# Scores and state products of a decayed linear attention on 32-column quarters of TensorE

## The chip, the cores and the metric

One core of a Trainium2 chip runs the whole kernel. The metric is the device time of one execution in microseconds (us); lower is better. A kernel is given by the median of its runs, and one execution is taken with a profile, from which every row below comes. TensorE is called PE, its weight loads PEld, VectorE DVE, ScalarE ACT, GpSimd POOL, and SyncE, which issues the transfers, SP.

## The reference

4 sequences, 8 heads, 768 tokens, head size 48. Each head carries a complex 48 x 48 state with a decay for each row and token, and the result goes through a two-layer network with a sigmoid gate:

```python
for t in range(S):
    new_re = ar * S_re - ai * S_im
    new_im = ar * S_im + ai * S_re
    kv = einsum('bhd,bhe->bhde', k[:, :, t], v[:, :, t])
    S_re, S_im = new_re + kv, new_im
    y[:, :, t] = einsum('bhd,bhde->bhe', q[:, :, t], S_re)
x = y as (3072 tokens, 384)
h = x @ w_in          # 384 x 2048
out = (h * sigmoid(1.702 * h)) @ w_out
```

## The kernel before, in words

**Tiling.** The 3072 tokens are 12 units of 256 tokens, three to a sequence; a unit has two chunks of 128 tokens (`c`), and a chunk handles 8 heads in two halves of four (`hh`). `prepare(u)` turns the decays of a unit into factors by scans, logarithms and sines on DVE and ACT, multiplies q and k by them, and sends the products by DMA into `qkh`, where each head has its 48 real parts in partitions 0 to 47 and its 48 imaginary parts in 64 to 111. `attend(u)` (L677 to L778) is the attention of a unit. `moe(n)` (L784 to L866) is the network, for a block of one or two units: `hidden` (L807, matmul at L814) and `project` (L833, matmul at L845). The first two blocks hold one unit and work in fp32; the other five hold two units and split each fp32 value into two fp32r parts, so that three products stand for one.

**The attention on TensorE.** Every fp32 matmul stands in the trace as two records, and each record has a weight load.
- `scores` (L702, matmul at L707): for each half of four heads, keys against queries. Keys come in two pieces of 64 (`x`); a piece's output stands in a 64-partition half of the PSUM tile `p_ps`, turned by head, and only queries from the first key of the piece on are computed: 128 columns for the first piece, 64 for the second. 8 matmuls, 16 records. DVE then multiplies by a causal mask (`pm`, L711), which has two layouts for the two ways in which the halves are turned.
- `mix` (L718, matmul at L733): values and old state against masked scores and queries, into `x_ps`; four heads each write their own 32 partitions. In three parts `r`, the last with twice the matmuls. ACT reads `x_ps` (L742), DVE the rest of it (L746).
- `turn` (L761, transpose at L763): two heads' keys transposed into `kz_ps`, copied by ACT to `kt` (L766).
- `zed` (L753, matmul at L757): transposed keys against values, the new state's products; each head has two matmuls of 48 weight columns, at output partitions 0 and 64. 8 matmuls, 16 records. DVE adds the result to the state `st` (L772, L776).

The instruction's form names the part of the array in use: 128\*128 and 112\*128 for the network and the transposes, 128\*64 for `scores`, 128\*48 for `zed`, 128\*32 for `mix`.

**Values.** `vts` holds the values of a chunk, padded, and behind them a second copy for the four odd heads, with rows rolled by 64 keys, so that they fit the turned scores. It is loaded by one DMA for each chunk (L699).

**The order of the work.** Nothing runs in the order in which it is written. `add(engine, duration, rank, function, r=, w=, kind=)` enters each step in a `Plan` with a duration written by hand and the names that it reads and writes. `order()` (L307) makes 100 rounds for each of 12 settings in `PARTS`: a forward list schedule over the five engines, a backward one for due times, ranks moved towards the due times; the order with the lowest modelled time is issued. The model charges PE `CHANGE` = 0.09 us where the next step's `kind` differs from the last one's; `stay` makes the choice of the next PE step prefer the same kind. Before the change there are two kinds: `"r"` for the fp32r network, and `None` for all else. `lag` (L83) is the delay from a step's end to its reader on another engine, 0.13 us, or 0.22 us if the reader is PE.

```python
for x in range(2):
    for j in range(4):
        h, lo = 4 * hh + j, HL * x
        to = HL * ((x + j) % 2)
        mm(p_ps[to : to + HL, j, lo:L], lhsT=at(h, 1, c)[:, lo : lo + HL], rhs=at(h, 0, c)[:, lo:L], ...)
```

Of the kernel before, what the change touches and what calls it, by code (L numbers as in the profile page):

```python
# [21 lines left out]
P = 128  # L22
L = 128
HL = 64
T = 256
# [28 lines left out]
SCRATCH = 1024  # L54

# [27 lines left out]
def lag(a, b):  # L83
    return LAG if b != "PE" else 0.0 if a == b else LAG_PE


class Plan:
# [31 lines left out]
    def forward(self, rank, stay):  # L119
# [10 lines left out]
        kinds, kind = self.kinds, None  # L130
# [5 lines left out]
        while done < len(ops):  # L136
# [29 lines left out]
            elif e == "PE":  # L166
                pick = min(can[e], key=lambda x: x[0] + (stay if kinds[x[1]] != kind else 0.0))
            else:
                pick = can[e][0]
# [16 lines left out]
            else:  # L186
# [92 lines left out]
    def time(self, order, load):  # L279
# [6 lines left out]
        kinds, kind = self.kinds, None  # L286
        for n in order:
# [11 lines left out]
            if e == "PE":  # L299
                dur += CHANGE if kinds[n] != kind else 0.0  # L300
                kind = kinds[n]
# [36 lines left out]
REMAP = 4.0  # L338
# [4 lines left out]
def attention_moe(ctx: ExitStack, tc: tile.TileContext, qk_in, v, a_in, w_in, w_out, qn, kn, vn, an, bn, out):  # L343
# [9 lines left out]
    mask = sb.tile([P, 2, P], F32, name="mask")  # L353
# [18 lines left out]
    vts = [sb.tile([P, H * VP + H // 2 * 2 * E0], F32, name=f"v{i}") for i in range(2)]  # L372
# [25 lines left out]
    nc.gpsimd.tensor_copy(out=mask[0:HL, 1, :], in_=mask[HL:P, 0, :])  # L398
    nc.gpsimd.tensor_copy(out=mask[HL:P, 1, :], in_=mask[0:HL, 0, :])
# [63 lines left out]
    def convert(n):  # L463
# [13 lines left out]
        add("SP", 2.19, rk - 4, lambda: dma(out=raw.bitcast(I32), in_=(w_in if m == "A" else w_out)[j].bitcast(I32)),  # L477
# [51 lines left out]
    def prepare_part(u, i, a, b, np_, mag, den, rec, sp, qm, th, *keys):  # L529
# [26 lines left out]
        z = 2 * C * P * 4 / 360e3  # L556
# [91 lines left out]
        for x, (dst, kd, fac, kf) in enumerate(((rv, "qr", cs, k_cs), (qv, "qk", t, k_th))):  # L648
# [3 lines left out]
            if u == i == 0 and x == 1:  # L652
                for k in range(WARM):
                    add("PE", 0.43, -WARM + k, lambda k=k, dst=dst: mm(  # L654
# [19 lines left out]
    def attend(u):  # L674
# [22 lines left out]
        for c in range(2):  # L697
            vt, kv = vts[c], f"v{c}"
            add("SP", 0.96, rk(4 * c) - 5, lambda vt=vt, c=c: dma(out=vt, in_=v[u, c]), w=[kv])  # L699
# [504 lines left out]
```

## Time and profile before

| | |
|---|---|
| median of 3 runs | 594.53 us (592.7 to 594.9) |
| the profiled execution | 593.85 us, its span 592.1 us |
| busy: PE, DVE, ACT, POOL | 94%, 79%, 47%, 4% of the span |
| records on PE | 4828, and as many weight loads |

A page of the profile gives the busy time of each engine, the chain of work that ended last, and groups of instructions by line with count, busy time and mean duration. Matmuls are pipelined, and a record's duration is longer than the step from its start to the next one's start; steps are therefore read from the timeline, as differences of starts. The timeline merges neighbouring records of one line and one pair of tiles, and shows one row with their count.

### The profile page before, as it was taken

How to read it: one execution, taken by the hardware profiler on the slowest of the kernel's cores; microseconds unless marked ns; L12 is line 12 of the kernel's file. 1: busy time of each engine (PE TensorE's matmuls, PEld its weight loads, DVE VectorE, ACT ScalarE, POOL GpSimd, SP SyncE). 2: the span in 40 equal slices, each digit the busy share in tenths (PEclk: the TensorE clock that was granted, in tenths of full speed). 3: DMA queues.
4: the chain of work that ended last, by engine and by line, in shares of the span. 5: the costliest groups of instructions: out<-in, count | busy, mean ns of one | idle time of the engine just before them, and what ended most of it. 6: DMA issues, size and time to landing. Idle time of an engine off the chain costs nothing.

```text
span 592.1 us, 11952 instructions
## 1 busy us (share of the span) xinstructions
PE 554.8 (94%) x4828; PEld 449.8 (76%) x4828; DVE 466.3 (79%) x826; ACT 276.4 (47%) x428; POOL 22.4 (4%) x75
## 2 busy tenths in 40 slices
PE   0389999999999999999999999999999999999997
PEld 0368888888788878787887787877787878878885
DVE  7999989988898977797978787977979954554333
ACT  7878677965537327237364246345346321111110
POOL 5001001000100000000000000000000000000000
PEclk9999999999999999999999999999999999999999
DMA  8478792747454192247085257286184372241111
GB/s 333 141 243 321 203 245 79 134 138 133 153 114 98 28 212 87 77 104 186 14 153 175 69 136 221 61 135 200 62 177 151 76 147 84 66 125 55 44 41 68
DMA packets 30890, 78.30 MB, mean 132 GB/s; under 512 B 4208, under 2 KB 7024, under 8 KB 30832
## 3 DMA queue, kind: packets, MB, share of 16 engines
q1 hardware_dynamic: 30832, 77.52, 48.8%
q8 instruction: 38, 0.62, 0.5%
q14 instruction: 20, 0.16, 0.1%
HBM read 53.87 MB, written 4.72 MB: 99 GB/s over the span
## 4 chain that ended last, share of the span: by engine, by line
PE 69%; DMA 13%; DVE 11%; ACT 3%; issue 2%; SPq 2%; DVEq 0%; ACTq 0%
PE h_ps L814 27%; PE o_ps L845 26%; PE x_ps L733 6%; DMA raw_w<-in_w_in_dram 4%; PE p_ps L707 4%; DMA raw_w<-in_w_out_dram 3%; PE kz_ps L763 3%; DMA raw<-in_w_out_dram 2%; PE kz_ps L757 2%; DMA raw<-in_w_in_dram 2%; DVE qk L461 1%; PE h_ps L654 1%; DMA qkh<-qr 1%; DVE pm L711 1%; DVE fit L877 1%
## 5 line engine op out<-in xcount | busy, mean ns | idle before, releaser
L826 ACT ACTIVATE g<-h_ps 128x512 f32<-128x512 f32 x80 | 47.4, 599 | 148.0 <-PE h_ps L814 138.8
L845 PE MATMUL o_ps<-gh,hiU 128*128 128x512 f32 x240 | 96.2, 401 | 0.0
L814 PE MATMUL h_ps<-xhi,hiA 128*128 128x512 f32 x240 | 95.6, 398 | 0.7 <-ACT xhi L742 0.6
L845 PE MATMUL o_ps<-gl,hiU 128*128 128x512 f32 x240 | 93.7, 391 | 0.0
L814 PE MATMUL h_ps<-xlo,hiA 128*128 128x512 f32 x240 | 93.6, 390 | 0.1
L845 PE MATMUL o_ps<-gh,loU 128*128 128x512 f32 x240 | 93.6, 390 | 0.0
L814 PE MATMUL h_ps<-xhi,loA 128*128 128x512 f32 x240 | 93.6, 390 | 0.0
L829 DVE CAST gh<-g 128x512 fp32r<-128x512 f32 x80 | 33.9, 424 | 43.5 <-PE o_ps L845 38.5
L766 ACT ACTIVATE kt<-kz_ps 128x224 f32<-128x224 f32 x80 | 28.4, 356 | 70.6 <-PE kz_ps L763 32.8
L877 DVE TENSOR_REDUCE fit<-raw_w 128x1 f32<-128x256 f32 x96 | 37.6, 413 | 29.2 <-DMA raw_w<-in_w_out_dram 16.2
L831 DVE TENSOR_TENSOR gl<-g,gh 128x512 fp32r<-128x512 f32 x80 | 55.1, 688 | 4.0
L845 PEld LDWEIGHTS o_ps<-gh,hiU 128*128 128x128 f32 x240 | 45.0, 188 | 11.2 <-issue 2.2
L814 PEld LDWEIGHTS h_ps<-xhi,hiA 128*128 128x128 f32 x240 | 45.0, 188 | 10.4 <-ACT xhi L742 0.9
L845 PEld LDWEIGHTS o_ps<-gl,hiU 128*128 128x128 f32 x240 | 45.1, 188 | 10.1 <-DVE gl L831 0.4
L814 PEld LDWEIGHTS h_ps<-xhi,loA 128*128 128x128 f32 x240 | 45.0, 188 | 9.5
L814 PEld LDWEIGHTS h_ps<-xlo,hiA 128*128 128x128 f32 x240 | 45.1, 188 | 9.1 <-DVE xlo L746 0.4
L845 PEld LDWEIGHTS o_ps<-gh,loU 128*128 128x128 f32 x240 | 45.1, 188 | 8.6
L845 PE MATMUL o_ps<-g,valU 128*128 128x256 f32 x192 | 47.1, 384 | 0.0
L461 DVE TENSOR_TENSOR qk<-qk,s 128x768 f32<-128x768 f32 (+1 forms) x52 | 45.5, 890 | 0.9 <-ACT s L647 0.6
L814 PE MATMUL h_ps<-x,valA 128*128 128x256 f32 x192 | 45.3, 380 | 0.3 <-ACT x L742 0.3
L1033 ACT ACT_TABLE_LOAD x35 | 44.9, 1283 | 1.4 <-PEq L1192 0.8
L707 PEld LDWEIGHTS p_ps<-qkh 128*64 128x64 f32 x768 | 36.2, 136 | 10.2 <-issue 4.6
(93 smaller groups left out, 853.4 us busy)
## 6 DMA issues: line engine op xcount, KB each, us to landing
v<-in_v_dram SPq DMA_DIRECT2D x24, 352.0 KB, 4.5
ri<-in_a_dram SPq DMA_DIRECT2D x11, 768.0 KB, 5.4
qk<-in_qk_dram SPq DMA_DIRECT2D x11, 768.0 KB, 5.0
qkh<-qr SPq DMA_DIRECT2D x22, 288.6 KB, 5.9
qkh<-qk SPq DMA_DIRECT2D x22, 288.6 KB, 6.9
raw<-in_w_in_dram SPq DMA_DIRECT2D x8, 768.0 KB, 6.7
raw<-in_w_out_dram SPq DMA_DIRECT2D x8, 768.0 KB, 7.6
raw_w<-in_w_in_dram SPq DMA_DIRECT2D x24, 256.0 KB, 3.7
```

The source lines that it names most:

```text
L461: add(en, t, rank, lambda: e.tensor_tensor(out=out, in0=a, in1=b, op=alu), **kw)
L707: mm(p_ps[to : to + HL, j, lo:L], lhsT=at(h, 1, c)[:, lo : lo + HL], rhs=at(h, 0, c)[:, lo:L], start=True, stop=True)
L733: mm(x_ps[32 * j : 32 * j + 32, r, :], lhsT=lt, rhs=rt, start=n == 0, stop=n == len(steps) - 1)
L763: nc.tensor.transpose(k_ps[:, j, :], at(4 * hh + 2 * e + j, 1, c)[0:KD], ident[0:KD, 0:KD])
L766: add("ACT", a_t(2 * KD) - 0.12, rk(4 * c + hh), lambda e=e: act(out=kt[0][:, 2 * e : 2 * e + 2, :], in_=k_ps, func=AF.Copy), r=["K"], w=[ ...
L814: mm(h_ps[hb][:, hs], lhsT=ww[:, r * T + f * P : r * T + (f + 1) * P], rhs=x[:, r, :], start=k == 0, stop=k == last)
L826: add("ACT", a_t(N) - 0.15, rk(i + f / 2), lambda hb=hb, hs=hs: act(out=g32[hb][:, hs], in_=h_ps[hb][:, hs], func=AF.Silu, scale=SLOPE), r ...
L829: add("DVE", d_t(N, 2), rk(i + f / 2), lambda hb=hb, hs=hs: dve.tensor_copy(out=high.g(hb)[:, hs], in_=g32[hb][:, hs]), r=regs("g", kf), w ...
L831: add("DVE", d_t(N), rk(i + f / 2), lambda hb=hb, hs=hs: dve.tensor_tensor(out=glo[hb][:, hs], in0=g32[hb][:, hs], in1=high.g(hb)[:, hs].b ...
L845: mm(o_ps[m][:, 0:N], lhsT=y[:, f * DM + m * P : f * DM + (m + 1) * P], rhs=x[:, hs], start=i == 0 and f == 0 and k == 0, stop=i == NP - 1 ...
L877: add("DVE", d_t(CK), rk + 2, lambda x=x, op=op: dve.tensor_reduce(out=f_w[:, x, n : n + 1], in_=weights.looked_at()[:, :, 1], op=op, axis ...
L1033: nc.scalar.preload_act_table_set(o[5])
```

## The change

Scores are computed in four pieces of 32 keys (`QL`) rather than two of 64; piece `x` of head `j` goes to the quarter `(x + j) % 4` of the partitions, and has queries from its first key on: 128, 96, 64 or 32 columns. The mask has four layouts, so `pm` is one plain product, and POOL makes them at the start by 12 copies rather than 2. Values have a rolled copy for the six heads whose scores are turned. `zed` has four matmuls for a head rather than two: weight columns 0 to 31 and 32 to 47 of the real and of the imaginary part. The planner has four kinds (`a` for the network and the warm-up, `t` for transposes, `m` for scores, mix, state products and the one small matmul of the final check; `s` is in its table and no step has it), a price for each change from one kind to another, delays by pair of engines, and some durations changed. `PIECES` has one piece, so `hidden` and `project` issue what they issued.

```diff
+QL = 32
+NQ = L // QL
 def lag(a, b):
-    return LAG if b != "PE" else 0.0 if a == b else LAG_PE
+    return LAGS.get((a, b), LAG)
-                pick = min(can[e], key=lambda x: x[0] + (stay if kinds[x[1]] != kind else 0.0))
+                pick = min(can[e], key=lambda x: x[0] + stay * CHANGE[kind, kinds[x[1]]])
-                    dur += CHANGE if kinds[n] != kind else 0.0
+                    dur += CHANGE[kind, kinds[n]]
-PARTS = tuple((x, y) for y in (0.0, 2.0, 5.0) for x in (0.4, 0.2, 0.1, 0.05))
-CHANGE = 0.09
+PARTS = tuple((x, y) for y in (0.0, 20.0, 50.0) for x in (0.4, 0.2, 0.1, 0.05))
+CHANGE = {(a, b): 0.0 for a in "atsm" for b in "atsm"}
+CHANGE |= {("a", "s"): 0.09, ("a", "m"): 0.085, ("t", "a"): 0.02, ("t", "s"): 0.07, ("t", "m"): 0.07, ("s", "t"): 0.1, ("s", "a"): 0.19}
+CHANGE |= {("s", "m"): 0.1, ("m", "s"): 0.115, ("m", "t"): 0.115, ("m", "a"): 0.205}
 LAG = 0.13
-LAG_PE = 0.22
+LAGS = {("PE", "PE"): 0.0, ("ACT", "PE"): 0.22, ("DVE", "PE"): 0.22, ("SP", "PE"): 0.22, ("POOL", "PE"): 0.22, ("PE", "ACT"): 0.25, ("PE", "DVE"): 0.17}
-REMAP = 4.0
+REMAP = 5.2
-    mask = sb.tile([P, 2, P], F32, name="mask")
+    mask = sb.tile([P, NQ, P], F32, name="mask")
-    vts = [sb.tile([P, H * VP + H // 2 * 2 * E0], F32, name=f"v{i}") for i in range(2)]
+    vts = [sb.tile([P, H * VP + 2 * (NQ - 1) * 2 * E0], F32, name=f"v{i}") for i in range(2)]
-    nc.gpsimd.tensor_copy(out=mask[0:HL, 1, :], in_=mask[HL:P, 0, :])
-    nc.gpsimd.tensor_copy(out=mask[HL:P, 1, :], in_=mask[0:HL, 0, :])
+    for j in range(1, NQ):
+        for x in range(NQ):
+            y = (x + j) % NQ
+            nc.gpsimd.tensor_copy(out=mask[y * QL : (y + 1) * QL, j, :], in_=mask[x * QL : (x + 1) * QL, 0, :])
-                    for x in range(2):
-                        for j in range(4):
-                            h, lo = 4 * hh + j, HL * x
-                            to = HL * ((x + j) % 2)
-                            mm(p_ps[to : to + HL, j, lo:L], lhsT=at(h, 1, c)[:, lo : lo + HL], rhs=at(h, 0, c)[:, lo:L],
+                    for x in range(NQ):
+                        for j in range(NQ):
+                            h, lo = NQ * hh + j, QL * x
+                            to = QL * ((x + j) % NQ)
+                            mm(p_ps[to : to + QL, j, lo:L], lhsT=at(h, 1, c)[:, lo : lo + QL], rhs=at(h, 0, c)[:, lo:L],
                                start=True, stop=True)
-                add("PE", 0.77, rk(4 * c + hh), scores, r=hk[c], w=["P"], name=f"P{u}.{c}.{hh}", work=0.97)
+                add("PE", 0.6, rk(4 * c + hh), scores, r=hk[c], w=["P"], name=f"P{u}.{c}.{hh}", work=0.97, kind="m")
-                    out=pm[hh].rearrange("p (a b) t -> p a b t", b=2), in0=p_ps.rearrange("p (a b) t -> p a b t", b=2),
-                    in1=mask.unsqueeze(1).to_broadcast([P, 2, 2, L]), op=ALU.mult
+                    out=pm[hh], in0=p_ps, in1=mask, op=ALU.mult
-                            if h % 2:
-                                lo = H * VP + h // 2 * 2 * E0 + (E0 if r < 2 else 0)
+                            if h % NQ:
+                                lo = H * VP + (h - 1 - h // NQ) * 2 * E0 + (E0 if (r < 2) == (h % 2 == 1) else 0)
-                        for x in range(2):
-                            mm(z_ps[64 * x : 64 * x + D, j * VP + lo : j * VP + lo + D], lhsT=kt[0][:, j, 64 * x : 64 * x + D],
+                        for a, b in ((0, E0), (HL, HL + E0), (E0, D), (HL + E0, HL + D)):
+                            mm(z_ps[a:b, j * VP + lo : j * VP + lo + D], lhsT=kt[0][:, j, a:b],
                                rhs=vt[:, h * VP + lo : h * VP + lo + D], start=True, stop=True)
-                add("PE", 0.495, rk(4 * c + 2 + hh), zed, r=["kt.0", "kt.1", kv], w=["Z"], work=0.49)
+                add("PE", 0.39, rk(4 * c + 2 + hh), zed, r=["kt.0", "kt.1", kv], w=["Z"], work=0.49, kind="m")
```

The planner's durations of `turn` (0.19 to 0.24), `mix` (0.46 and 1.0 to 0.436 and 0.872), the value load (0.96 to 0.87), the weight load from memory (2.19 to 1.9) and the decay load also change; the host lays out the values with the longer rolled copy.

## Rows read from the trace of the kernel before

**Rows 1.** Page, part 1: busy us, share of the span, instructions, by engine.
```profile
PE 554.8 (94%) x4828; PEld 449.8 (76%) x4828; DVE 466.3 (79%) x826; ACT 276.4 (47%) x428; POOL 22.4 (4%) x75
```
**Rows 2.** Page, part 4: the chain that ended last, shares by engine.
```profile
PE 69%; DMA 13%; DVE 11%; ACT 3%; issue 2%; SPq 2%; DVEq 0%; ACTq 0%
```
**Rows 3.** Stretches: length, busy us (count) of each engine, PE's granted clock, DMA.
```profile
24.00:160.00 136.00, 132.56 (x1308) 109.92 (x1308) 125.76 (x192) 96.49 (x151) 8.72 (x22) 1.00 0.65 185
160.00:360.00 200.00, 198.76 (x1731) 160.11 (x1730) 167.36 (x282) 93.60 (x137) 3.28 (x20) 1.00 0.46 112
360.00:460.00 100.00, 97.26 (x871) 77.74 (x870) 86.25 (x162) 45.54 (x67) 2.52 (x15) 1.00 0.55 141
...
522.00:592.00 70.00, 65.84 (x290) 53.79 (x289) 29.20 (x68) 9.60 (x16) 0.00 (x0) 1.00 0.21 62
```
**Rows 4.** PE timeline at 332 us: start, length, engine, line, tiles, shape, records.
```profile
332.39 0.89 PE L707 MATMUL p_ps<-qkh 128*64 128x128 f32 x16
333.11 0.53 PE L757 MATMUL kz_ps<-v,kt 128*48 128x48 f32 x16
333.57 0.43 PE L733 MATMUL x_ps<-pm,v 128*32 128x128 f32 x8
333.81 0.40 PE L733 MATMUL x_ps<-qkh,st 128*32 128x128 f32 x8
334.14 0.50 PE L845 MATMUL o_ps<-gh,hiU 128*128 128x512 f32 x1
334.48 0.39 PE L845 MATMUL o_ps<-gh,loU 128*128 128x512 f32 x1
```
**Rows 5.** PE timeline at 281 us: state products, then scores.
```profile
281.30 0.56 PE L757 MATMUL kz_ps<-v,kt 128*48 128x48 f32 x16
281.69 0.86 PE L707 MATMUL p_ps<-qkh 128*64 128x128 f32 x16
```
**Rows 6.** PE timeline at 193 us: two parts within a mix.
```profile
192.96 0.40 PE L733 MATMUL x_ps<-pm,v 128*32 128x128 f32 x8
193.18 0.40 PE L733 MATMUL x_ps<-qkh,st 128*32 128x128 f32 x8
```
**Rows 7.** Groups by line and shape: count | busy us, mean ns | idle before.
```profile
L877 DVE TENSOR_REDUCE fit<-raw_w 128x1 f32<-128x256 f32 x96 | 37.6, 413 | 29.2 <-DMA raw_w<-in_w_out_dram 16.2 <-DMA raw_w<-in_w_in_dram 13.0
...
L757 PE MATMUL kz_ps<-v,kt 128*48 128x48 f32 x640 | 22.3, 212 | 0.1
```
**Rows 8.** One stretch inside a mix: PE busy (x), PEld busy (x), other engines.
```profile
333.56:333.62 0.06, 0.06 (x8) 0.05 (x8) 0.06 (x1) 0.00 (x0) 0.00 (x0) 1.00 0.00 0
```
**Rows 9.** PE timeline: first and last direct change between mix and the other two.
```profile
36.17 0.42 PE L733 MATMUL x_ps<-pm,v 128*32 128x128 f32 x8
36.69 0.56 PE L757 MATMUL kz_ps<-v,kt 128*48 128x48 f32 x16
...
515.76 0.89 PE L707 MATMUL p_ps<-qkh 128*64 128x128 f32 x16
516.58 0.42 PE L733 MATMUL x_ps<-pm,v 128*32 128x128 f32 x8
```
**Rows 10.** PE timeline at 303 us: from the network into state products.
```profile
302.80 0.39 PE L845 MATMUL o_ps<-gh,loU 128*128 128x512 f32 x1
303.02 0.39 PE L845 MATMUL o_ps<-gl,hiU 128*128 128x512 f32 x1
303.34 0.56 PE L757 MATMUL kz_ps<-v,kt 128*48 128x48 f32 x16
```
**Rows 11.** Timeline of the first 13 us: POOL and DVE.
```profile
3.99 0.29 POOL L399 COPY mask<-mask 64x128 f32<-64x128 f32 x1
...
7.86 0.14 POOL L576 MEMSET s<- 128x3 f32 x2
...
12.12 1.05 DVE L587 TENSOR_TENSOR_SCAN s<-s,s 128x129 f32<-128x129 f32 x3
```
**Rows 12.** Transfers: count, KB each, median us from issue to landing.
```profile
v<-in_v_dram SPq DMA_DIRECT2D x24, 352.0 KB, 4.5
```

More of the change, by code (lines that the diff above doesn't have):

```diff
@@ L54 @@
 SCRATCH = 1024
+PIECES = ((0, 1, 2),)
 LOGS = "natural_log_exp_and_others"
@@ L285, in time @@
         clock = Clock()
[L286 removed]
+        kinds, kind = self.kinds, "a"
         for n in order:
@@ L475, in ti @@
             return weights.whole(m, j).bitcast(I32)
-        add("SP", 2.19, rk - 4, lambda: dma(out=raw.bitcast(I32), in_=(w_in if m == "A" else w_out)[j].bitcast(I32)),
+        add("SP", 1.9, rk - 4, lambda: dma(out=raw.bitcast(I32), in_=(w_in if m == "A" else w_out)[j].bitcast(I32)),
             w=[kg, kl], name=f"f{n}")
@@ L698, in attend @@
             vt, kv = vts[c], f"v{c}"
-            add("SP", 0.96, rk(4 * c) - 5, lambda vt=vt, c=c: dma(out=vt, in_=v[u, c]), w=[kv])
+            add("SP", 0.87, rk(4 * c) - 5, lambda vt=vt, c=c: dma(out=vt, in_=v[u, c]), w=[kv])
             skip = last and c == 1
@@ L735, in attend @@
             for r in range(NR):
-                add("PE", (0.46 if r < 2 else 1.0) * (1 if have else 0.5), rk(4 * c + 2), lambda r=r, mix=mix: mix(r),
-                    r=[kv, *hk[c], f"st{src}.{r}", f"pm{r}"] if r < 2 else [kv, *hk[c], f"st{src}.0", f"st{src}.1", "pm0", "pm1"], w=["x"], work=0.72)
+                add("PE", (0.436 if r < 2 else 0.872) * (1 if have else 0.5), rk(4 * c + 2), lambda r=r, mix=mix: mix(r),
+                    r=[kv, *hk[c], f"st{src}.{r}", f"pm{r}"] if r < 2 else [kv, *hk[c], f"st{src}.0", f"st{src}.1", "pm0", "pm1"], w=["x"], work=0.72, kind="m")
             b = BLOCK_OF[u] % 2
@@ L810, in hidden @@
                         terms = [(hi, high.x(n)[:, :, 0:N]), (hi, xlo[b][:, :, 0:N]), (lo, high.x(n)[:, :, 0:N])]
-                    k, last = 0, NR * len(terms) - 1
-                    for r in range(NR):
-                        for ww, x in terms:
-                            mm(h_ps[hb][:, hs], lhsT=ww[:, r * T + f * P : r * T + (f + 1) * P], rhs=x[:, r, :], start=k == 0, stop=k == last)
-                            k += 1
+                    for r in rs:
+                        for k, (ww, x) in enumerate(terms):
+                            mm(h_ps[hb][:, hs], lhsT=ww[:, r * T + f * P : r * T + (f + 1) * P], rhs=x[:, r, :],
+                               start=r + k == 0, stop=r == NR - 1 and k == len(terms) - 1)
                 cols = [f"{y}A{i}" for y in both_halves]
-                add("PE", NR * terms_of * columns, rk(i + f / 2 - 0.5), hidden, r=xk + cols, w=regs("h", kf), name=f"H{n}.{i}", work=0.975, kind=None if whole else "r")
+                for rs in PIECES:
+                    add("PE", len(rs) * terms_of * columns, rk(i + f / 2 - 0.5), lambda rs=rs, hidden=hidden: hidden(rs), r=xk + cols, w=regs("h", kf), name=f"H{n}.{i}", work=0.975, kind="a")
             for f in range(2):
@@ L851, in moe @@
             else:
-                parts = [((f,), tuple(range(NR))) for f in range(2)]
+                parts = [((f,), ms) for f in range(2) for ms in PIECES]
             for fs, ms in parts:
@@ L855, in moe @@
                     r=[k for y in (("gh",) if whole else ("gh", "gz")) for f in fs for k in regs(y, at(f)[2])] + cols, w=[f"o{m}" for m in ms],
-                    name=f"O{n}.{i}", work=0.975, kind=None if whole else "r")
+                    name=f"O{n}.{i}", work=0.975, kind="a")
         spent = [f"x{y}{b}.{c}" for y in "hl" for c in range(4)]
@@ L1168, in _layout @@
     vp[:, :, :, 1::2, VP - E0 :] = vv[:, :, :, 1::2, 0:E0]
-    vo = np.zeros((b * s // T, 2, L, h // 2, 2 * E0), dtype=va.dtype)
-    vo[..., 2 * E0 - d :] = np.roll(vp[:, :, :, 1::2, VP - d :], HL, axis=2)
+    vo = np.zeros((b * s // T, 2, L, h, 2 * E0), dtype=va.dtype)
+    for n in range(h):
+        at = slice(0, d) if n % 2 == 0 else slice(2 * E0 - d, 2 * E0)
+        of = slice(0, d) if n % 2 == 0 else slice(VP - d, VP)
+        vo[:, :, :, n, at] = np.roll(vp[:, :, :, n, of], n % NQ * QL, axis=2)
+    vo = vo[:, :, :, [n for n in range(h) if n % NQ]]
     vp, vo = (x.reshape(b * s // T, 2, L, -1) for x in (vp, vo))
```

14 lines of the change are left out of this document (7 added, 7 removed).

## The prediction

> **What bounds the kernel now.** First the busy shares: PE 94%, DVE 79%, ACT under half [rows 1]. The chain agrees, 69% of it is PE [rows 2], but a chain names only one path, so the stretches decide [rows 3]. From 160 to 360 us PE is busy for 198.76 of 200 us, in the weakest stretch, 360 to 460, still 97.26 of 100, and the last 70 us hold nothing but the last block's network and its output. [...] PE is the bound from its first record to its last. What it saves is worth its full price as long as the others can feed it. DVE is the next: 125.76 of 136 us up to 160, and 86.25 of 100 from 360 on [rows 3].
>
> So the sum is one of PE steps, read from start to start.
>
> **How long a set of records takes.** Scores are followed directly by state products after 333.11 - 332.39 = 0.72 us [rows 4]; state products by scores after 281.69 - 281.30 = 0.39 [rows 5]. Within a mix, 8 records of 128 columns take 193.18 - 192.96 = 0.22 [rows 6]; four quarters work side by side, so a set of four takes 0.109. In state products the 16 records last 0.53 in all and one lasts about 0.21 [rows 4, 7]: 0.32 from first to last start, in pairs (two 64-partition halves), so seven steps of 0.045 for 48 columns. A line through both points gives 6.6 ns + 0.8 ns a column for a set, be it of two or four. It can be tried on the old scores: four pairs of 128 and four of 64 columns make 4 x 0.109 + 4 x 0.058 = 0.67, and 0.05 to get going gives the 0.72 seen.
>
> **Scores.** There are 48 groups (24 chunks, two halves) of 16 records [rows 4]. After the change a group has 32 records, in two sets of four for each of 128, 96, 64 and 32 columns: 2 x (0.109 + 0.083 + 0.058 + 0.032) = 0.56, and 0.02 to get going as a mix has it (0.24 for its first 8 records against 0.22 [rows 4, 6]). 0.58 for 0.72 saves 0.14, and 48 x 0.14 = **-6.7 us**. It is a saving because four pieces leave out more of the masked triangle: 320 columns in each of four quarters for 384 in each of two halves. The nearest rows know no set of four below 128 columns. Bounds: all sets as the line has it, -6.7; no set shorter than what state products need for as many records (16 in 0.36, so 22.5 ns a record and 0.09 for four), 2 x (0.109 + 3 x 0.09) + 0.02 = 0.78, +2.8. I take the line, since within a mix eight weight loads and four matmuls start inside 0.06 us [rows 8], 5 ns apart, and the shortest set asks for eight in 32.
>
> **State products.** 640 records at 16 a group [rows 7] are 40 groups. They go from 16 records to 32, but each quarter still streams 48 columns eight times: eight sets of 0.045, as before. **0 us**. Bound above: at 22.5 ns a record 0.72 for 0.36, 40 x 0.36 = +14.4; below, nothing, since no column is saved.
>
> What hides the doubled records is that four run side by side. [...]
>
> **Changes of form.** Leaving scores costs 516.58 - 515.76 = 0.82 for 0.72, so 0.10 [rows 9, 4], and what follows loses another 0.02 to 0.05 in starting. Reading the whole PE timeline, mix follows scores or state products directly 17 times and they follow mix 8 times, the first and the last in [rows 9]. All will have one form: 17 x 0.126 + 8 x 0.165 (a mix is left 0.33 after its last set of 8 started, 0.11 more than 0.22 [rows 4, 6], and 0.05 to start scores) = **-3.5 us**. Scores and state products go over to the network some 57 times, and will leave as a mix does, at 0.11 to 0.12 for 0.10, taken as 0.015 dearer: **+0.9 us**.
>
> **The new order.** A way out and back costs 0.10 (303.34 - 303.02 = 0.32 for the 0.22 between network records) + 0.02 + 0.11 + 0.12 (334.48 - 334.14 = 0.34 for 0.22) = 0.35 us [rows 10, 4]. There are 90 of them in the PE timeline. The old planner charged 0.09 at a change of precision alone, none between fp32 network and attention; the new one charges each close to the steps above. Ten trips fewer would be -3.5; ten more, if the search settles badly, +3.5. I take five fewer, **-1.7 us**, a choice and not a measurement.
>
> **What costs nothing.** Ten more mask copies of some 0.3 us and a mask twice as wide (0.3) hold POOL 3.7 us longer at the start. Their cover is the wait for the first scan: the small memsets that it needs ended at about 8.0, and it starts at 12.12 [rows 11], so 0.4 us are left; without that cover the first q and k would come late by the overrun, at most a few tenths. The value load grows from 704 to 832 columns, 352 to 416 KB [rows 12], 24 times 64 KB = 1.5 MB. SP issues it five slots ahead, and at 4.5 us to landing a sixth more is 0.8; what is queued behind it on SP are the remaps of q and k, due units later. The masking product keeps its shape. PE's instructions rise by 768 + 640 records and as many loads over 4828 each [rows 1]; if fetching them lagged, it would show as the 22.5 ns above.
>
> **Sum.** -6.7 + 0 - 3.5 + 0.9 - 1.7 = -11.0 us. The profiled execution took 593.85 us (span 592.1), so 582.9; its time is 0.7 below the median of the runs shown, which gives 583.5 us.
>
> **Rivals.**
> *Records have a floor.* The one that ends slower. Its place is the 32-column sets in scores and state products; its price, at the fastest sustained rate that any row shows (22.5 ns a record), is +2.8 + 14.4 - 3.5 + 0.9 = +14.6, so 609 us. For it: no run of 16 records in the trace goes faster. Against: at 128 and 64 columns the columns explain the time alone, and [rows 8] shows bursts four times as dense. It decides from about 16 ns a record on: there state products cost 40 x (0.51 - 0.36) = +6.0, scores 48 x (0.66 - 0.72) = -2.9, and the rest -2.6. [...] Chance 0.06. Of it the rule's own floor has 0.02, since a row already breaks it.
> *The feeders give out.* DVE is at 92% up to 160 us and 86% from 360 to 460 [rows 3]. These are 236 of the 498 us in which attention runs. If PE waits there for what it saves, half of the -11 goes: 589 us. Against: DVE's looking through the weights to check them, 413 ns for each of 96 reductions [rows 7], can move to the last 70 us, where DVE is busy for 29 of 70 [rows 3]. Chance 0.15.
> *The planner's order eats it.* The longer modelled delays make the search hold work back, ten trips more and some waits: -11.0 + 1.7 + 3.5 + 4 = -2, so 592.5. Chance 0.06.
> *It doesn't do what it says.* If sets of unequal length hold each other up, scores keep 0.72 and only the changes of form go: -4.3, so 590. Chance 0.05.
>
> **How the numbers follow.** The forecast has 0.68 and spans 580 (ten more trips saved) to 587. The range reaches 578 to 590: down for a search that does better, up over the feeders and unequal sets. Left out are floor, bad order and tails, about 0.18. A measurement of this kernel can tell about 0.5% (3 us) from no change. Faster: 0.68 + 0.15 + 0.05 = 0.88, less a little for mixed cases, 0.87; same 0.07; slower 0.06.
>
> **What would show it.** In the profile after: scores followed directly by a state product or mix step in 0.58 to 0.60 us, state products in 0.39 to 0.40, no extra 0.1 between these and the mix, PE still over 97% busy from 160 to 360, the first scan at about 12.1, and PE's steps in scores down by some 6 to 7 us in all. I am wrong if 32 records of state products take 0.5 us or more, if PE shows new waits on DVE's `pm` or on ACT's `kt`, or if the trips between network and attention rise above 90.

## The result and the profile after

The changed kernel takes 587.66 us (median of 17 runs) for 594.22 us before (17 runs): a ratio of 0.9891, 95% interval 0.9866 to 0.9916, so 1.1% faster. The forecast was 583.5 us with a range of 578 to 590. Two of the 17 executions after the change (3064 and 706 us) were disturbed: the ratio leaves them out, and without them the median would be 587.62 us. The profiled execution took 586.36 us, its span is 584.6 us; that is 7.5 us of span less than before, where 11.0 were forecast.

Page of the changed kernel, part 1 (busy us, share of the span, instructions, by engine), and the instruction queue of part 3 (packets, MB, share):

```profile
PE 540.1 (92%) x6236; PEld 445.1 (76%) x6236; DVE 470.1 (80%) x826; ACT 275.6 (47%) x428; POOL 27.4 (5%) x85
q8 instruction: 49, 0.80, 0.6%
```

Its stretches, to be read against [rows 3]: length, busy us (count) of PE, PEld, DVE, ACT, POOL, PE's granted clock, DMA share, GB/s.

```profile
24.00:160.00 136.00, 124.64 (x1682) 105.48 (x1686) 127.55 (x196) 97.22 (x154) 7.28 (x22) 0.99 0.64 186
160.00:360.00 200.00, 196.98 (x2353) 160.50 (x2342) 180.99 (x308) 99.89 (x145) 5.94 (x25) 1.00 0.52 130
360.00:460.00 100.00, 98.69 (x1256) 80.98 (x1255) 77.94 (x145) 40.87 (x64) 1.75 (x10) 1.00 0.52 131
```

PE is still the bound, but less wholly so: up to 160 us it is idle for 11.4 of 136 us, where it was 3.4, and 2.6 of these lie ahead of its first record. In the later stretches it is over 98% busy, and DVE, the feared neighbour, is not the limit at the end: 77.94 us from 360 to 460, where it was 86.25. Most of the loss is in the first quarter, and the sum of the whole has to be drawn up in PE's steps.

**What a group takes.** PE timeline of the changed kernel at 243 us: start, length, engine, line, tiles, shape, records.

```profile
243.52 0.35 PE L769 MATMUL kz_ps<-ident,qkh 112*128 112x112 f32 x2
243.81 0.77 PE L714 MATMUL p_ps<-qkh 128*32 128x128 f32 x32
244.39 0.41 PE L739 MATMUL x_ps<-pm,v 128*32 128x128 f32 x8
244.61 0.40 PE L739 MATMUL x_ps<-qkh,st 128*32 128x128 f32 x8
244.83 0.53 PE L763 MATMUL kz_ps<-v,kt 128*32 128x48 f32 x32
245.17 0.41 PE L739 MATMUL x_ps<-pm,v 128*32 128x128 f32 x8
```

As before, the column to subtract is the first. Scores: 244.39 - 243.81 = 0.58 us for 32 records, the forecast to the hundredth. State products: 245.17 - 244.83 = 0.34 us for 32 records, where 0.39 to 0.40 were to be seen. And from scores to mix, from mix to state products and back there is no step of 0.1 more: scores, mix and half of the records of the state products stand in the form 128\*32, the other half in 128\*16 (the row at 49.40 below).

**The sum of PE's steps**, start to start over the whole timeline, in us:

| | before | after |
|---|---|---|
| first PE record starts | 24.09 | 26.60 |
| from the first to the start of the last PE record | 563.7 | 553.7 |
| scores / state products / mix | 40.1 / 19.1 / 50.6 | 35.9 / 18.7 / 44.1 |
| transposes / network / warm-up | 24.2 / 421.6 / 8.0 | 23.7 / 424.0 / 7.3 |
| of all these: waits | 18.6 | 27.3 |
| trips between network and attention forms | 90 | 61 |
| direct changes of form between mix and scores or state products | 25 | 0 |

"Waits" is here what the groups (neighbouring records of one line) took from their start to the next group's start beyond the shortest group of the same line and length with the same follower. It holds idle time, stops within a group and the loss where the granted clock is below 1.00; a group without its like counts nothing. "Trips" are the entries into scores, mix or state products from the network, the warm-up or the transposes.

So the steps themselves fell by 10.0 + 8.7 = 18.7 us; 8.7 came back as waits and 2.5 as a later start: -18.7 + 8.7 + 2.5 = -7.5, the span. The forecast foresaw a smaller first number and nothing of the other two.

**The later start.** Timeline of the changed kernel's first 14 us (engine, line, operation; in brackets idle time and releaser), and its first PE record:

```profile
3.86 4.99 POOL L406 COPY mask<-mask 32x128 f32<-32x128 f32 x12
8.91 3.52 POOL L410 MEMSET qkh<- 128x4104 f32 x1
9.99 2.86 DVE L487 TENSOR_SCALAR valA<-raw 128x768 int32<-128x768 int32 x1 [1.48 <-DMA raw<-in_w_in_dram]
12.40 0.49 POOL L583 MEMSET s<- 128x3 f32 x1
13.70 1.05 DVE L594 TENSOR_TENSOR_SCAN s<-s,s 128x129 f32<-128x129 f32 x3
26.60 7.44 PE L661 MATMUL h_ps<-qk,ident 128*128 128x256 f32 x26 [26.60 <-DVE qk L468]
```

And of the kernel before:

```profile
4.34 3.53 POOL L403 MEMSET qkh<- 128x4104 f32 x1
8.71 0.56 DVE L480 TENSOR_SCALAR valA<-raw 128x768 int32<-128x768 int32 x1 [1.06 <-DMA raw<-in_w_in_dram]
```

The 12 copies take 4.99 us (0.42 each). The big memset that follows ran from 4.34 to 7.87 before; now it runs from 8.91 to 12.43, and a DVE operation that took 0.56 us stands beside it for 2.86, until 12.85, just behind its end. The small memsets that the scan needs come behind the big one and end at 12.89. The first scan starts at 13.70 for 12.12 [rows 11], with no idle time of DVE before it: it is DVE's held-up operation, and not these memsets, that makes it late.

**The new stops.** PE timeline of the changed kernel at 46 and 144 us; "issue" in brackets is idle time in which PE waited for nothing that the profile shows.

```profile
46.55 0.43 PE L763 MATMUL kz_ps<-v,kt 128*32 128x48 f32 x20
49.40 0.35 PE L763 MATMUL kz_ps<-v,kt 128*16 128x48 f32 x12 [2.41 <-issue]
...
144.37 0.70 PE L851 MATMUL o_ps<-g,valU 128*128 128x256 f32 x2
146.11 1.13 PE L851 MATMUL o_ps<-g,valU 128*128 128x256 f32 x4 [1.04 <-issue]
```

PE stops in the middle of a group, with all its inputs there, at the first stop after 20 of 32 records. What it lacks is instructions. PE has 2 x 1408 = 2816 instructions more than before (records and weight loads), and the instruction queue moved 49 packets for 38 ([rows 1] has the counts before; the page before shows 38 packets, 0.62 MB). 2816 / 11 = 256: by these counts a packet holds 256 instructions, and 0.80 MB / 49 = 16 KB. The two stops lie 8 x 256 instructions apart (the 706th and the 2754th of PE's queue). Transfers of the changed kernel from 40 to 50 us (packets, MB, share of the 16 engines' time):

```profile
q1 hardware_dynamic: 1002, 3.93, 98.6%
q8 instruction: 1, 0.02, 0.7%
```

The packet due here begins at 47.05, with the transfer engines full of the kernel's own data, and lands at 48.11 (1.06 us). PE goes on at 49.40. The one of the second stop begins at 143.66, takes 1.23 us, and PE goes on at 146.11. A third, short one lies 256 before the first, at the 450th: PE goes on at 41.93, 1.26 us after its packet (39.26 to 40.67). Beyond the shortest step the three cost 2.62, 1.21 and 0.34, so 4.2 us. The kernel before had none: there every packet landed at least 3.05 us before PE came to the place where these stops lie (256 k + 194). And a stop has a tail, seen in the stretch from 44 to 60 us: the granted clock is 0.89 there, 0.50 from 50.4 to 53.7 us and 1.00 in the rest; it fell 0.9 to 1.0 us after PE had gone on (49.40).

```profile
44.00:60.00 16.00, 13.43 (x158) 11.30 (x150) 15.96 (x26) 9.18 (x15) 1.79 (x3) 0.89 0.80 304
```

Last, PE's waits for other engines, by releaser (us, count, longest), in the changed kernel and, in the last two rows, before:

```profile
PE kz_ps L769 <- ACT kt L772: 4.1, 5, 1.5
PE p_ps L714 <- DVE pm L718: 2.8, 5, 0.8
PE x_ps L739 <- DVE pm L718: 0.8, 3, 0.4
...
PE x_ps L733 <- DVE pm L711: 3.3, 3, 1.6
PE kz_ps L763 <- ACT kt L766: 2.4, 4, 1.0
```

Behind its first record PE's idle time is 13.2 us after the change and 8.2 before. Without the stops for instructions (3.5) it is 9.7, so 1.5 more than before.

### The profile page after: what moved, and what is told of

Same layout as the page of the kernel before. It is cut to its first block, busy times and chain, and to the rows that moved or that the text cites. A ratio compares the mean times of both kernels' runs of the same rounds, so it can differ in the third digit from the quotient of the medians.

```text
span 584.6 us, 14786 instructions
## 1 busy us (share of the span) xinstructions
PE 540.1 (92%) x6236; PEld 445.1 (76%) x6236; DVE 470.1 (80%) x826; ACT 275.6 (47%) x428; POOL 27.4 (5%) x85
## 4 chain that ended last, share of the span: by engine, by line
PE 66%; DVE 4%; issue 1%; ACT 1%; DMA 1%; DVEq 0%
PE o_ps L851 27%; PE h_ps L819 27%; PE x_ps L739 5%; PE p_ps L714 3%; PE kz_ps L769 2%; PE kz_ps L763 2%; DVE pm L718 1%; DMA raw_w<-in_w_in_dram 1%; DVE loU L511 0%; DVE qk L468 0%; DVE qr L468 0%; DVE gl L837 0%; DVE gh L835 0%; ACT kt L772 0%; DVE xlo L752 0%
## 5 line engine op out<-in xcount | busy, mean ns | idle before, releaser
L835 DVE CAST gh<-g 128x512 fp32r<-128x512 f32 x80 | 33.8, 423 | 43.2 <-PE o_ps L851 39.3
L851 PEld LDWEIGHTS o_ps<-gl,hiU 128*128 128x128 f32 x240 | 45.1, 188 | 10.2 <-DVE gl L837 0.6
L819 PE MATMUL h_ps<-x,valA 128*128 128x256 f32 x192 | 47.7, 392 | 0.0
L718 DVE TENSOR_TENSOR pm<-p_ps,mask 128x512 f32<-128x512 f32 x48 | 33.1, 690 | 15.7 <-PE p_ps L714 14.5
```

Of the source, the lines that this page charges most:

```text
L718: add("DVE", d_t(CW), rk(4 * c + hh), lambda hh=hh: dve.tensor_tensor(out=pm[hh], in0=p_ps, in1=mask, op=ALU.mult), r=["P"], w=[f"pm{hh}"])
L819: mm(h_ps[hb][:, hs], lhsT=ww[:, r * T + f * P : r * T + (f + 1) * P], rhs=x[:, r, :], start=r + k == 0, stop=r == NR - 1 and k == len(ter ...
L835: add("DVE", d_t(N, 2), rk(i + f / 2), lambda hb=hb, hs=hs: dve.tensor_copy(out=high.g(hb)[:, hs], in_=g32[hb][:, hs]), r=regs("g", kf), w ...
L851: mm(o_ps[m][:, 0:N], lhsT=y[:, f * DM + m * P : f * DM + (m + 1) * P], rhs=x[:, hs], start=i == 0 and f == 0 and k == 0, stop=i == NP - 1 ...
```

## The experiments

The theory: the short sets do what the forecast said; the gain that went missing was lost at the start (copies ahead of the big memset), to late instructions, and to waits of the new order. Rivals: that the new forms themselves cost something, or that the whole gain is the planner's and none the matmuls'. A time is the median, with the range and count of its runs, and a ratio stands against the kernel before.

### 1. The mask copies later

```diff
-    for j in range(1, NQ):
-        for x in range(NQ):
-            y = (x + j) % NQ
-            nc.gpsimd.tensor_copy(out=mask[y * QL : (y + 1) * QL, j, :], ...)
+        def ends():
+            pool.tensor_copy(out=fa, in_=w(sp)[:, :, 0])
+            if u == 0 and i == 1:
+                for j in range(1, NQ):
+                    for x in range(NQ):
+                        y = (x + j) % NQ
+                        pool.tensor_copy(out=mask[y * QL : (y + 1) * QL, j, :], ...)
+        add("POOL", 0.13, rk("qm"), ends, ...)
```

The change with its order kept; the copies move behind the first scans.

> The changed kernel with its 12 mask copies moved on POOL from the start to behind the second look at the first unit's scans (about 18 us in); order of all else unchanged. Theory (POOL's queue is late at the start): the big memset and the small ones that the first scan needs end some 5 us earlier, the first PE record comes at about 24.1 us instead of 26.6, and the time falls by 2 to 3 us, to 584.5 to 585.5. Rival (the new order on DVE and ACT makes the start late): first PE record stays at 26.6, time stays at 587.7.

Measured: 587.44 us (585.97 to 589.48, 6 runs), ratio 0.9868 (0.9834 to 0.9902): no different from the change itself. Timeline of its start:

```profile
9.75 0.56 DVE L483 TENSOR_SCALAR valA<-raw 128x768 int32<-128x768 int32 x1 [1.28 <-DMA raw<-in_w_in_dram]
11.17 1.05 DVE L590 TENSOR_TENSOR_SCAN s<-s,s 128x129 f32<-128x129 f32 x3
19.45 0.84 ACT L440 ACTIVATE s<-ri 128x768 f32<-128x768 f32 x1 [2.50 <-DVE qk L464]
```

Neither expectation held whole. DVE's operation is back to 0.56 us and the scan comes 2.5 us earlier, at 11.17. PE's first record comes only 1.1 us earlier, at 25.46 and not at 24.1: the rest of the delay is the new order, which puts a step of the next unit (the activation at 19.45, waiting 2.50 us) ahead on ACT. And the 1.1 us do not reach the end. Its PE timeline at the first and at the long stop, and the stretch from 44 to 60 us:

```profile
42.02 0.27 PE L718 MATMUL p_ps<-qkh 128*32 128x32 f32 x7 [1.39 <-issue]
46.43 0.43 PE L767 MATMUL kz_ps<-v,kt 128*32 128x48 f32 x20
49.55 0.51 PE L767 MATMUL kz_ps<-v,kt 128*16 128x48 f32 x12 [2.69 <-issue]
...
44.00:60.00 16.00, 13.16 (x144) 10.85 (x135) 15.96 (x26) 7.07 (x13) 1.79 (x3) 0.79 0.74 281
```

The lead is lost at the first stop: the last record before PE's 450th instruction starts at 40.44, 1.15 us earlier than in the change, but PE goes on at 42.02 (41.93 there), since the packet landed at 40.80 (40.67). At the long stop PE was only 0.12 us ahead, stood until 49.55 (49.40 in the change itself), and the clock fell further, to 0.79 in the stretch. PE was waiting for arrivals that did not move with it.

### 2. The kernel before with ten more copies

```diff
+    for n in range(10):
+        q = n % 4 * 32
+        nc.gpsimd.tensor_copy(out=pm[0][q : q + 32, n // 4, :], in_=mask[q : q + 32, 0, :])
```

> The kernel before with ten extra copies of 32 partitions on POOL at the start, into a buffer that is overwritten later; nothing else changed. Theory (POOL's queue): the first PE record moves from 24.1 to about 26, the time rises by about 2 us, to 596. Rival (the new order): nothing waits for POOL there, first PE record stays at 24.1, time stays at 594.2.

Measured: 597.74 us (593.83 to 601.7, 12 runs), ratio 1.0055 (1.0029 to 1.0082). Its start, from the profiled execution:

```profile
8.79 3.52 POOL L406 MEMSET qkh<- 128x4104 f32 x1
9.46 0.55 DVE L567 SCALAR_TENSOR_TENSOR s<-ri,s 128x384 f32<-128x384 f32 x1
9.93 0.55 DVE L464 TENSOR_TENSOR s<-ri,s 128x384 f32<-128x384 f32 x1
10.40 2.18 DVE L580 TENSOR_SCALAR s<-s 128x384 f32<-128x384 f32 x1
24.44 2.05 PE L657 MATMUL h_ps<-qk,ident 128*128 128x256 f32 x4 [24.44 <-DVE qk L464]
```

Another DVE operation (0.42 us without the memset beside it) is held for 2.18 us, until just behind the memset's end at 12.31: the hold-up shows in a kernel that has nothing else of the change. It does not meet every operation: the two before it, with two inputs each, run beside the same memset in 0.55 us, their usual time. But PE starts only 0.35 us later than before, and the profiled execution, at 593.83, is as fast as before, while the median rose by some 3 us. The profile explains the first tenths and not the rest; that stays open.

### 3. The old matmuls with the new planner

The planner's part of the change (its price table, delays, durations) on the old matmuls, told what these cost: scores 0.72, state products 0.395, both of the kind `s`.

```diff
-                add("PE", 0.77, rk(4 * c + hh), scores, ..., work=0.97)
+                add("PE", 0.72, rk(4 * c + hh), scores, ..., work=0.97, kind="s")
-                add("PE", 0.495, rk(4 * c + 2 + hh), zed, ..., work=0.49)
+                add("PE", 0.395, rk(4 * c + 2 + hh), zed, ..., work=0.49, kind="s")
```

> The matmuls of the kernel before (scores on halves, state products of 48 columns), ordered by the new planner with its prices by form, delays and durations (scores 0.72, state products 0.395, both kind s). Theory (one form for all is what lets the order be better): direct changes between mix and the others stay, trips between network and attention fall from 90 to 80 at best, and the time is 590 to 593. Rival (the prices alone do it): trips fall to 65 or fewer and the time is 586 to 588.

Measured: 592.77 us (591.55 to 593.56, 12 runs), ratio 0.9965 (0.9946 to 0.9984), some 2 us faster than before. Trips fell from 90 to 74, worth 16 x 0.35 = 5.6, but PE starts at 24.84 and its waits rose from 18.6 to 23.3. A planner that counts the changes of form does save trips; more than half of the saving comes back as waits. The time is what the theory expected, with fewer trips than it allowed for; the rival's 586 to 588 is out.

### 4. The new matmuls with the old planner

The planner's part undone in the changed kernel, with scores put down at 0.63.

```diff
-                add("PE", 0.6, rk(4 * c + hh), scores, ..., work=0.97, kind="m")
+                add("PE", 0.63, rk(4 * c + hh), scores, ..., work=0.97)
-                add("PE", 0.39, rk(4 * c + 2 + hh), zed, ..., work=0.49, kind="m")
+                add("PE", 0.495, rk(4 * c + 2 + hh), zed, ..., work=0.49)
```

> The matmuls of the changed kernel, ordered by the planner of before (one price of 0.09 between two precisions, its delays and durations, scores 0.63). Theory (the forecast's own terms without the better order): 6.7 us less for scores, 2.6 for the changes of form, 2 to 2.5 back at the start: 587 to 588, with about 90 trips. Rival (the gain is the planner's): 592 to 594.

Measured: 608.16 us (604.13 to 616.62, 6 runs), ratio 1.0203 (1.0158 to 1.0248). Both expectations missed. The trace does not put it on the matmuls: groups of scores and of state products followed by a mix take 0.58 and 0.36 us, in the change 0.58 and 0.34. It is the order that the search found: 93 trips, and waits of 39.3 us. One of them, in its PE timeline at 489 us, and the stretch around it:

```profile
493.49 0.63 PE L767 MATMUL kz_ps<-ident,qkh 112*128 112x112 f32 x2 [3.56 <-ACT kt L770]
494.37 0.63 PE L817 MATMUL h_ps<-xlo,hiA 128*128 128x512 f32 x1
494.80 0.63 PE L817 MATMUL h_ps<-xhi,loA 128*128 128x512 f32 x1
...
484.00:500.00 16.00, 12.44 (x159) 9.71 (x158) 4.88 (x12) 2.79 (x7) 0.00 (x0) 0.79 0.40 100
```

PE waits 3.56 us for ACT's `kt`, and after that network records start 494.80 - 494.37 = 0.43 us apart where they take 0.22 [rows 10]: the granted clock of the stretch is 0.79. This run does not price the old planner. It shows that orders of the same matmuls can lie 20 us apart, and that a comparison between two searches says little of what was changed beside them. The next runs therefore keep one order.

### 5. State products on 48 columns again, same order

```diff
-                        for a, b in ((0, E0), (HL, HL + E0), (E0, D), (HL + E0, HL + D)):
-                            mm(z_ps[a:b, ...], lhsT=kt[0][:, j, a:b],
+                        for x in range(2):
+                            mm(z_ps[64 * x : 64 * x + D, ...], lhsT=kt[0][:, j, 64 * x : 64 * x + D],
```

> The changed kernel, in its own order, with the state products on 48 columns again (16 records a group). Theory (quartering them gains nothing in streaming, only the same form as their neighbours): a group alone keeps 0.36 to 0.40, but the 45 places where it stands next to scores or mix cost 0.13 each, +5.9 us; 1280 PE instructions fewer give back 2 to 3 of the stalls in which PE has nothing to run: 590 to 592 us. Rival (their records are the load on instruction fetch, and that weighs more): 584 to 586.

Measured: 587.3 us (586.22 to 594.45, 12 runs), ratio 0.9895 (0.986 to 0.9931): the same as the change. Its PE timeline at the place of the long stop:

```profile
47.20 0.40 PE L739 MATMUL x_ps<-qkh,st 128*32 128x128 f32 x8
47.54 0.56 PE L763 MATMUL kz_ps<-v,kt 128*48 128x48 f32 x16
```

Two things cancel. The changes of form are back: 47.54 - 47.20 = 0.34 for a part of the mix that takes 0.22 where the form stays. Over the kernel PE's steps without waits rise from 526.5 to 532.7 us, by 6.2, close to the 5.9 that were expected for 45 such places; state products alone go from 15.5 to 19.8. (With waits they go from 18.7 to 20.1 only, since the 18.7 hold the long stop.) And the stops are gone, with 1280 instructions and five packets fewer (44 for 49); the waits fall from 27.3 to 22.1, by 5.2.

### 6. The old matmuls in the changed kernel's order

The matmuls, masks and values of before, issued in exactly the order of the changed kernel: the planner keeps the changed kernel's durations and kinds.

```diff
-                        for x in range(NQ):
-                            for j in range(NQ):
-                                h, lo = NQ * hh + j, QL * x
+                        for x in range(2):
+                            for j in range(4):
+                                h, lo = 4 * hh + j, HL * x
...
                 add("PE", 0.6, rk(4 * c + hh), scores, ..., work=0.97, kind="m")
```

> All matmuls, masks and values of the kernel before, in exactly the order that the changed kernel issues. Theory (sum of the terms at one order): scores +6.7, 69 direct changes of form at 0.14 +9.6, start -1 to -2, stalls for want of instructions and the clock behind them -4 to -6: 595 to 599 us. Rival (the order is the whole gain): 585 to 588.

Measured: 593.54 us (589.69 to 597.73, 12 runs), ratio 0.9974 (0.9937 to 1.0011), between the two expectations. In one and the same order the new matmuls are thus worth some 5 us: the ratios differ by 0.9974 - 0.9891 = 0.0083, which by the two intervals is 4.9 us, give or take 2.7. In the median the order alone does next to nothing for the old ones. The first PE record is at 25.37, with the two old copies: of the 2.5 us of later start about 1.3 (25.37 - 24.09) are the order's, and about 1.2 (26.60 - 25.37) the copies'. The profiled execution is slower than the median (span 595.8) and had a granted clock of 0.91 in one stretch, so its waits are not used, and its steps only without them:

```profile
60.00:100.00 40.00, 35.35 (x285) 29.01 (x285) 31.55 (x46) 24.00 (x36) 1.10 (x5) 0.91 0.78 201
```

Without waits PE's steps take 538.4 us here, for 545.1 before and 526.5 in the change. Of the 18.7 us from before to the change, 6.7 thus come with the order and 11.9 with the matmuls (rounded). The forecast's prices say much the same. The order has 29 trips fewer (-10.2), but with the old matmuls 55 direct changes of form for 25 (30 x 0.14 = +4.2): -6.0. The matmuls save 6.7 in scores and 55 x 0.14 = 7.7 in form, and pay 0.9: -13.5. That the medians show 4.9 us of the 11.9 fits the copies (1.2) and the stops (4.2), which only the new matmuls have, and the clock behind the stops.

### 7. Fewer instructions, same order

```diff
-                        for a, b in ((0, E0), (HL, HL + E0), (E0, D), (HL + E0, HL + D)):
+                        for a, b in ((0, E0), (HL, HL + E0)):
```

The 16-column matmuls of the state products are left out, 1280 PE instructions; forms and order stay.

> The changed kernel, in its own order, with the 16-column matmuls of the state products left out (the last 16 of 48 rows of each half of the state are then wrong); a group streams as long as before, on two quarters rather than four, with 16 records fewer. Theory (PE stops because its instructions have not arrived): the stops at 46.8 us (2.6 us) and 144.7 us (1.4) go or shrink, the clock stays up behind them, and the time falls by 3 to 5 us to 583 to 585. Rival (PE stops for a transfer or a neighbour's result): stops and time stay, 587 to 588.

Measured: 584.09 us (582.68 to 589.19, 6 runs), ratio 0.9826 (0.9782 to 0.9869), as the theory of late instructions had it. Its PE timeline at the place of the long stop, and the stretch:

```profile
47.16 0.52 PE L763 MATMUL kz_ps<-v,kt 128*32 128x48 f32 x16
47.60 0.41 PE L769 MATMUL kz_ps<-ident,qkh 112*128 112x112 f32 x2
...
44.00:60.00 16.00, 15.94 (x172) 13.62 (x169) 15.96 (x26) 13.05 (x22) 1.79 (x3) 1.00 0.76 288
```

No stop, and in this stretch the clock at 1.00 for 0.89. The clock is not won for the whole profiled execution, though: from 36 to 44 us it is at 0.79 here (1.00 in the change), which loses about as much (8 x 0.21 = 1.7 us, for 16 x 0.11 = 1.8), behind waits of 1.06 and 0.57 us for ACT's `kt`; experiment 5 shows the same 0.79 there. By the medians the edit is worth 3.6 us; by the two intervals 0.0065 of the time, 3.9 us, give or take 3.0. None of it is shorter work: state products take 15.6 us for 18.7, but of these 3.1 the long stop was 2.6, and PE's steps without waits take 527.0 us in all, for 526.5. The profiled execution shows less of it than the medians (585.39 us, 1.0 below that of the change), since PE waits there once for ACT's `g` (1.3 us) and once for DVE's `xlo` (1.2), which it didn't in the change: part of what the stops gave back was taken by the next engine that was late.

### 8. A planner that counts instructions

The copies later, and a model in the planner: it counts PE's instructions, lets each packet of 256 arrive 4 us after it is asked for, and makes steps dearer that would run dry.

```diff
+class Fetch:
+...
+        while 256 * len(self.at) + 153 < self.n + count:
+            self.at.append(... + FETCH)
...
+FETCH, DRY = 4.0, 5.0
```

> The changed kernel with its mask copies later and with a planner that counts PE's instructions: after 256 k + 153 of them the next 256 are asked for, they come 4 us later, and a step that needs them waits; among ready steps it shuns one that would wait. Theory (the stops come from dense runs of small matmuls): the search spreads them, no stop over 1 us behind 60 us, 581 to 584 us. Rival (the arrival hangs on how full the transfer queues are, not on PE's order): stops of the same sum, 586 to 588.

Measured: 591.86 us (587.55 to 595.83, 12 runs), ratio 0.9948 (0.9918 to 0.9977); neither expectation held. Two stops of over 1 us stayed, at 86 and 391 us, and this is the PE timeline at the longer one:

```profile
392.71 0.95 PE L768 MATMUL x_ps<-pm,v 128*32 128x128 f32 x25 [1.61 <-issue]
```

One fixed delay of 4 us, the author's estimate, did not say when these packets came. PE did start early, at 23.67, and waits are no more than in the change (26.1 for 27.3), but the new order's steps without waits are longer, 531.1 for 526.5. The profiled execution took 587.55 us; why the median lies 4 us higher its trace does not show.

### 9. Experiments 1 and 5 together, same order

State products on 48 columns and the copies later, in the changed kernel's order.

> Both at once, in the changed kernel's order: state products on 48 columns, and the mask copies moved behind the start. Theory (the earlier start was lost in the later mask copies alone because PE's next instructions still landed at the same moment; with 1280 fewer that stop is gone): the first PE record at 25.4 us as there, no stop over 1 us for instructions, and the start's 1.2 us come through: 585.5 to 586.5. Rival (the start is hidden for another reason): 587.3, as with the state products alone.

Measured: 585.7 us (584.96 to 590.56, 6 runs), ratio 0.986 (0.9827 to 0.9893), inside what was expected. First PE record, and the place of the long stop:

```profile
25.57 2.05 PE L665 MATMUL h_ps<-qk,ident 128*128 128x256 f32 x4 [25.57 <-DVE qk L464]
...
45.54 0.56 PE L767 MATMUL kz_ps<-v,kt 128*48 128x48 f32 x16
...
44.00:60.00 16.00, 15.49 (x128) 13.30 (x129) 15.96 (x26) 12.70 (x21) 1.91 (x3) 1.00 0.81 303
```

With no stop to absorb it, the earlier start is kept: the state products' group stands at 45.54 where experiment 5 had it at 47.54, and the span is 583.3 us for 585.7, the median 1.6 us below. Of these 2.0 us 1.1 are the start (25.57 for 26.66); most of the rest is the clock, at 0.79 from 36 to 44 us in the profile of experiment 5 and at 1.00 here. Of the versions that compute the whole result this is the fastest in the median; its interval overlaps those of the change and of experiment 5, so it is a likely gain and not a proven one.

### 10. Experiment 9 with an order of its own

```diff
-                add("PE", 0.39, rk(4 * c + 2 + hh), zed, ..., kind="m")
+                add("PE", 0.395, rk(4 * c + 2 + hh), zed, ..., kind="s")
```

> Mask copies later and state products on 48 columns, with the planner told so (kind s, 0.395 us) and free to choose its order. Theory (with the price of 0.1 known the search puts state products where a change is paid anyway): 584 to 586. Rival (every new order has its own waits, 2 to 4 us either way): anything from 585 to 592.

Measured: 590.57 us (589.66 to 592.86, 6 runs), ratio 0.9923 (0.9899 to 0.9948). Told the truth about the state products' form, the search came to 66 trips and, in the profiled execution (592.86 us), waits of 29.9 us. It lost nearly 5 us to the order that it was given in experiment 9. The rival held: the new order brought its own waits.

## Why the prediction was right, and where its steps were not

**The sign and the range** held: 587.66 lies between 578 and 590. The median gained 6.6 us for 11.0 forecast (7.5 in the profiled execution).

**Scores, right.** 0.58 for 0.72 us, so 48 x 0.14 = 6.7. Experiment 6, one order with old and new matmuls, gives 4.9 us (2.2 to 7.6) for the matmuls as a whole; as state products come to nothing (experiment 5), that is the scores and their changes of form, less what their instructions cost. PE's steps in scores fell by 4.2 us over the kernel, not by the 6 to 7 named as a sign; without waits they fell from 37.2 to 29.4, by 7.8, which holds the changes of form.

**State products, right in time, and with a price that was not in the step.** 0.34 us for 32 records is 10.6 ns a record. The floor of 22.5 ns is refuted for these tiles, in four quarters of the array, and no run shows the rule's own floor to which the forecast gave 0.02. But their doubled records brought the kernel 1280 instructions, five packets, and the stops; what they saved in form was given back, which experiment 5 shows.

**Direct changes of form, right.** 25 were to go and 25 went. Experiment 5, which puts a change of form back at 45 places, pays 6.2 us for them, 0.14 each, as priced.

**The new order, the step that failed.** "I take five fewer, -1.7 us, a choice and not a measurement": the trips fell by 29, to 61, at 0.35 us each worth 10.2 us. With this term in its measured size, the forecast's own prices give -6.7 - 3.5 + 0.9 - 10.2 = -19.5, and the timelines show -18.7 for the steps without their waits. So the prices were right and the count was far off; experiment 6 splits the 18.7 between order and matmuls, and the prices hold in both parts. Had nothing else happened, the kernel would stand near 575 us, below the range.

**What costs nothing, the other step that failed.** Three costs took 11.2 us of it back (8.7 and 2.5).
- *The start*: "at most a few tenths" was 2.5 us. The copies took 0.42 us each and not 0.3; the step measured their cover on POOL alone and did not ask what the big memset behind them would now run beside. The first scan, expected at 12.1, came at 13.70. About 1.2 us is the copies', about 1.3 the order's, which the step had not listed at all.
- *Instructions*: "if fetching them lagged, it would show as the 22.5 ns above" was wrong in kind. The late packets stopped PE three times, for 2.62, 1.21 and 0.34 us, and did not slow each record: 32 records of state products without a stop took 0.34 us. The stops cost 4.2 us, from nothing before, and behind the long one the granted clock fell to 0.50 for 3.3 us (50.4 to 53.7). Experiment 7 removes them and its median is 3.6 us lower.
- *Waits*: 8.7 - 4.2 = 4.5 us of what is left. PE's idle time on other engines rose by 1.5 of these: on ACT's `kt` from 2.4 to 4.1, on DVE's `pm` from 3.3 to 3.6, less on the rest. Both were named as signs of being wrong; only the first is new in size, and DVE's load from 360 to 460 is less than before, so "the feeders give out" did not happen. The rival "the planner's order eats it" had waits of this kind at 4 us and trips that rise; the trips fell. The other 3.0 us are not idle time. At the granted clock of 0.89 from 44 to 60 us PE lost at most 16 x 0.11 = 1.8; the rest is spread over many steps and not explained.

**A right number for partly wrong reasons.** The forecast came out 4 us low of the median because an underrated gain (18.7 for 11.0, so 7.7 us) and unseen costs of a like size (11.2) met; that they did is luck. What was priced by rows of the trace held; what was chosen without a row was off, in both directions.

**Still open:** why the median of experiment 2 rose by 3 us where its profile shows 0.35; why the median of experiment 8 lies 4 us above its profiled execution; and what sets how long a packet takes to come. The changed kernel's trace says this much: its last two packets begin, at 539.16 and 568.40, when PE has started 256 k + 153 and 256 k + 155 instructions, with few other transfers under way. The packet of the long stop began 5.95 us after PE had come to such a place (256 + 153, at 41.10), with the transfer engines 98.6% full. Counted from there, the delay is 3.1 us on the mean for the 19 packets with these engines at least 80% busy in the 2 us that followed, and 1.1 for the 22 with at most 40%. No kernel was tried with emptier queues at that place, so that the transfers are the cause is not shown.

## What to carry to other kernels

Price the instructions themselves: where narrow tiles double the records for the same columns, count PE's instructions in packets and look for idle time under "issue" in the middle of a group, since a gain in form can go back whole (experiment 5). When the order comes out of a search, try a matmul change with the order held fixed and the order change with the matmuls held fixed, because two searches differ by more than most edits (experiments 4, 8, 10). Before putting work on an engine at the start "in its idle time", look at what it pushes back and what that then runs beside.

## What was not expected of the hardware

- A GpSimd memset of 3.52 us held up VectorE until it ended: a TENSOR_SCALAR of 0.56 us that started 1.1 us into it took 2.86, and beside the same memset in experiment 2 another of 0.42 took 2.18; they ended 0.4 and 0.3 us behind it. Not every operation was held: a SCALAR_TENSOR_TENSOR and a TENSOR_TENSOR, with two inputs, ran beside the memset in 0.55 us (experiment 2). Why the ones were held and the others not, no run shows.
- PE's instructions came in packets of 256 (2816 more instructions, 11 more packets; 1280 fewer, 5 fewer). At the three stops of the changed kernel PE went on 1.2 to 1.3 us after the packet had landed (40.67 to 41.93, 48.11 to 49.40, 144.89 to 146.11).
- Idle times of 2.4 to 3.6 us were followed by a stretch at a lower granted clock (0.89 from 44 to 60 us in the changed kernel, with 0.50 from 50.4 to 53.7, and 0.79 in experiments 1 and 4), so such a stop cost more than its own length. The clock fell behind shorter ones too: in experiments 5 and 7 behind two waits of 1.0 and 0.6 us at 36 to 37 us, while waits of 1.46 and 0.57 at the same place in the changed kernel left it at 1.00. What decides is not shown.
